# Second head mixing in four 64x64 quarters with one op a visit, and three single PSUM banks for scores, mixing and values

## The chip, the cores and the metric

The kernel runs on one core of one Trainium2 chip. The metric is the device time of one execution in microseconds, from three executions. One more execution was profiled; all rows below come from its trace. TensorE runs the matrix products (PE in the rows, with its weight loads as PEld), VectorE is DVE, ScalarE is ACT, GpSimd is POOL, and SyncE (SP) issues the DMAs.

## The reference, cut to what matters

Talking-heads attention over 4 batches, 12 heads, 448 tokens and head size 64, then two dense layers. The change touches the attention alone.

```
scores = scale * np.matmul(q, k.transpose(0, 1, 3, 2))
scores = np.einsum('bhij,hg->bgij', scores, w_pre)
scores = scores - np.max(scores, axis=-1, keepdims=True)
attn = np.exp(scores)
attn = attn / (np.sum(attn, axis=-1, keepdims=True) + 1e-09)
attn = np.einsum('bhij,hg->bgij', attn, w_post)
return np.matmul(attn, v).astype(np.float32)
...
h = x @ w_in
g = h * np.cos(h)
return (g @ w_out).astype(np.float32)
...
h = np.maximum(np.maximum(x @ w1, x @ w2), x @ w3)
return (h @ w_out).astype(np.float32)
```

The heads are mixed twice, before the softmax with w_pre (here the first mixing) and after it with w_post (the second mixing).

## The kernel before, in words

The 448 query rows of a batch are cut into four score blocks of 100, 120, 120 and 108 rows (110 with padding), so there are 16 score blocks in all. For each block `qk` (line 674) makes the scores of a pair of heads as two products in the two halves of TensorE's rows; `evac` copies each head from PSUM to a tile `s` (6 of them), and `send` moves it by DMA into the tile `t` (2 of them), where the rows of 12 heads lie together: 60 partitions (5 query rows x 12 heads) in each half of the partitions. `new_t` first fills the 4 spare partitions with zeros by a DMA.

A **visit** works on two slices of `t`. `mix1` (line 701) multiplies 64x64 quarters of it with the block-diagonal `w1`; all four quarters of TensorE take one product each. The result is one or two **blocks** of 128 partitions x 448 keys (there are 92 visits, 88 with two sides and 4 with one, and 180 blocks). For each block `rowmax` (706), `soft` (711, the exponential with its row sum), `guard` (715), `recip` (719) and `wscale` (723, the small matrix `w2s` = w_post over the row sum) follow, and then `mix2` (728): the exponentials are the weights, 112 keys at a time, and `w2s` with 120 columns streams through, so that one bank `aps` of PSUM holds 4 x 120 columns, keys on the partitions. `keep` copies it into `a2`. When the two score blocks of a half batch are done, `av` (752) multiplies `a2` with the values `v`, `keepx` copies the result out, and `out` sends it to `xT` in DRAM, which the dense layers read.

PSUM has eight banks here: `ps_m` 2 (first mixing), `ps_t` 2 (second mixing), `ps_s` 2 and `ps_x` 2 (a ring of four for scores and values; a score bank from `ps_x` has the name `mps` in the rows, as a bank of `ps_m` has). `qk` and `av` are planned two pairs of heads at a time.

No order is written by hand. Class `Plan` takes every step with a rank, the engines that may do it with a time that the author gives it, the steps it needs, and the rings of buffers it takes; `Plan.run` goes through time with these figures and so fixes the order of each engine's instructions and, for copies, whether ACT or DVE does them. Each engine then works strictly in that order. A changed figure, rank or ring changes the order of everything in the attention.

Of the kernel before, what the change touches and what calls it, by code (L numbers as in the profile page):

```python
# [21 lines left out]
RI = 10  # L22
# [7 lines left out]
BUFS = {"k": 10, "q": 9, "s": 6, "e": 4, "w2s": 3, "v": 7, "xs": 3, "a2": 2, "ps_m": 2, "ps_t": 2, "ps_s": 2, "ps_x": 2}  # L30
# [481 lines left out]
class Plan:  # L512
# [17 lines left out]
    def run(self, places):  # L530
# [8 lines left out]
        while open_:  # L539
            best = {}  # L540
            for key in open_:
                rank, run, engines, after, takes, _ = self.ops[key]
                t = max([done[x] for x in after], default=-50.0)
                for ring in takes:
                    if len(taken[ring]) >= places[ring]:
                        last = self.frees[ring, taken[ring][-places[ring]]]
                        t = max([t] + [done.get(x, 1e9) for x in last])
# [15 lines left out]
            for ring in takes:  # L563
                taken[ring].append(key)
# [17 lines left out]
def attention(ctx, tc, q, k, v, w_pre, w_post, same_row, xT, tp, mlps):  # L582
# [8 lines left out]
        pool("v", BUFS["v"]), pool("xs", BUFS["xs"]), pool("a2", BUFS["a2"]))  # L591
# [11 lines left out]
    own = const.tile([128, RH], F32, name="own")  # L603
    zero = const.tile([PAD, S], F32, name="zero")
    w1 = const.tile([128, 64], F32, name="w1")
    w2t = const.tile([128, H, RI], F32, name="w2t")
    for x in (zero, wraw, blk, w1):
        nc.vector.memset(x, 0.0)

# [18 lines left out]
    def wmix(x, _):  # L628

        w = wraw[:, x, :]  # L630
        if x == 0:
            nc.vector.tensor_scalar(w, w, 1.0 / math.sqrt(D), None, op0=ALU.mult)
            nc.vector.tensor_add(own, blk[:, 0, :RH], blk[:, 0, RH:])
            nc.vector.tensor_mul(
                w1[:, :PH].rearrange("p (r g) -> p r g", g=H), w.unsqueeze(1).to_broadcast([128, RH, H]),
                own.unsqueeze(2).to_broadcast([128, RH, H]))
        else:
            nc.vector.tensor_mul(
                w2t, w.unsqueeze(2).to_broadcast([128, H, RI]), blk[:, 1, :].unsqueeze(1).to_broadcast([128, H, RI]))
# [11 lines left out]
    def vget(b, hp, _):  # L651
        live["v", b, hp] = vp.tile([JC, JB, 2, D], F32, name="v")
        nc.sync.dma_start(live["v", b, hp], v[b, hp])


    def pairs(x):
        return 2 * x, 2 * x + 1
# [9 lines left out]
    def qk(n, x, _):  # L667
        b, i0, m, _ = score[n]
        for hp in pairs(x):
            both = [score_psum(), score_psum()]  # L670
            for g, ps in enumerate(both):
                half = slice(64 * g, 64 * g + 64)
                live["s", n, 2 * hp + g] = ps
                nc.tensor.matmul(ps[:m], live["q", b, hp][half, i0:i0 + m], live["k", b, hp][half], start=True, stop=True)  # L674
# [18 lines left out]
    def mix1(v, _):  # L693
        n, u, sides = visits[v]
        i = blocks.index((n, u, 0))
        for a in sides:
            live["m", i + a] = ps_m.tile([128, S], F32, name="mps")
        for y in range(2):
            for a in sides:
                k = slice(64 * a, PAD + (a + 1) * PH)  # L700
                nc.tensor.matmul(live["m", i + a][64 * y:64 * y + 64], w1[k], live["t", n][k, 2 * u + y, :],  # L701
                                 start=True, stop=True)

    def rowmax(i, _):
        nm = live["nm", i] = st.tile([128, 1], F32, name="nm")
        nc.vector.tensor_reduce(nm, live["m", i], axis=AX.X, op=ALU.max, negate=True)  # L706

    def soft(i, _):
        e = live["e", i] = ep.tile([128, S], F32, name="e")
        z = live["z", i] = st.tile([128, 1], F32, name="z")  # L710
        nc.scalar.activation(e, live["m", i], AF.Exp, bias=live["nm", i], scale=1.0, accum_out=z)  # L711

    def guard(i, _):
        z = live["z", i]
        nc.vector.tensor_scalar(z, z, 1e-9, None, op0=ALU.add)

    def recip(i, _):
        rz = live["rz", i] = st.tile([128, 1], F32, name="rz")
        nc.vector.reciprocal(rz, live["z", i])
# [15 lines left out]
    def keep(i, eng):  # L735
        n, u, a = blocks[i]
        half = n // 2
        if ("a2", half) not in live:
            live["a2", half] = ap_.tile([JC, JB, H, NHALF], F32, name="a2")
        hi = score[n][3][1]  # L740
        o = (n % 2) * score[n - 1][2] + 2 * u * RH + (a * RH * hi if 2 * u < hi else RH * hi)
        copy(eng, live["a2", half][:, :, :, o:o + RI], live["a", i][:JC])


    def av(n, x, _):
        m, a2 = score[n - 1][2] + score[n][2], live["a2", n // 2]
        for hp in pairs(x):
            vt = live["v", score[n][0], hp]
            ps = live["av", hp] = score_psum()
            for j in range(JB):  # L750
                for g in range(2):
                    nc.tensor.matmul(ps[64 * g:64 * g + 64, :m], vt[:, j, g, :], a2[:, j, 2 * hp + g, :m],  # L752
                                     start=j == 0, stop=j == JB - 1)

    def keepx(n, hp, eng):
# [4 lines left out]
        for x in (n - 1, n):  # L760
            _, i0, m, (lo, hi) = score[x]
            o = i0 - half_of(n)[0]
            for halves, nt in ((2, hi), (1, lo - hi)):
                m = halves * RH * nt
                if nt:
                    copy(eng, xs[:, o:o + m].rearrange("p (a r t) -> p a r t", r=RH, t=nt),
                         ps[:, c:c + m].rearrange("p (a t r) -> p a r t", r=RH, t=nt))
# [6 lines left out]
    before, visit = {}, {}  # L774
# [15 lines left out]
    for n in range(NS):  # L790
        b = score[n][0]
        start, end = n % per == 0, n % per == per - 1
        for x in range(HP // 2):
# [362 lines left out]
```

## Time and profile before

| what | value |
|---|---|
| time, median of 3 executions | 1344.89 us (1341.59 to 1346.52) |
| profiled execution, its own time | 1346.08 us |
| its span, first to last instruction | 1344.3 us |
| PE busy | 94% of the span |
| DVE busy | 72% |
| ACT busy | 48% |
| granted TensorE clock, mean | 0.972 |

The kernel has two parts. The attention takes the first 530 us or so. After that the dense layers run, with PE busy all the time. A busy PE is no PE at its peak: a product counts as busy until its last result is out, while the next one already streams.

### The profile page before, as it was taken

The numbers are of one execution on the slowest core, as the hardware profiler recorded it, in microseconds if no ns is written. First come the engines' busy times: TensorE is split into PE (matmuls) and PEld (weight loads), VectorE is DVE, ScalarE is ACT, GpSimd is POOL, SyncE is SP. The second block draws the span as 40 slices with busy tenths as digits, with TensorE's granted clock in tenths as the row PEclk, the third lists the DMA queues.
The fourth block names the chain that finished last, engine by engine and source line by source line (L and its number), as shares of the span: only waits on it lengthen the run. The fifth ranks groups of instructions, "written<-read, shape, count | busy, mean of one in ns | idle before, by whom it ended". The sixth has DMA issues, their size and how long they took to land.

```text
span 1344.3 us, 20559 instructions
## 1 busy us (share of the span) xinstructions
PE 1266.5 (94%) x7182; PEld 1007.6 (75%) x7182; DVE 964.9 (72%) x2167; ACT 650.2 (48%) x1452; POOL 187.9 (14%) x170
## 2 busy tenths in 40 slices
PE   5889998999899887899999999999999999999998
PEld 2455555555556555699999999999999998989998
DVE  1565665667475669699999999999786544956455
ACT  2444453445344456577456555555554444344440
POOL 0000000000000012100000000000105645266450
PEclk7889999899899999899999999999999999999999
DMA  5744354435225333555444444444101212222112
GB/s 167 197 132 121 93 163 118 125 100 162 85 79 149 102 128 111 167 160 142 118 131 128 119 130 139 120 124 122 42 1 59 73 52 77 85 80 83 48 53 83
DMA packets 86031, 146.83 MB, mean 109 GB/s; under 512 B 9672, under 2 KB 68904, under 8 KB 85928
## 3 DMA queue, kind: packets, MB, share of 16 engines
q1 hardware_dynamic: 85928, 145.52, 37.1%
q8 instruction: 57, 0.93, 0.3%
q14 instruction: 46, 0.38, 0.1%
HBM read 84.96 MB, written 20.45 MB: 78 GB/s over the span
## 4 chain that ended last, share of the span: by engine, by line
PE 78%; DMA 9%; DVE 4%; ACT 3%; issue 2%; SPq 2%; POOL 1%; ACTq 0%; DVEq 0%; POOLq 0%
PE ps L165 18%; PE ps L167 18%; PE ps L166 18%; PE aps L728 10%; DMA t<-s 6%; PE mps L701 6%; PE ps L752 3%; PE mps L752 2%; PE ps L674 2%; PE mps L674 2%; ACT e L711 1%; POOL w L309 1%; DMA wf<-w 1%; DMA x<-xT 1%; DVE nm L706 1%
## 5 line engine op out<-in xcount | busy, mean ns | idle before, releaser
L165 PE MATMUL ps<-x,w 128*128 128x448 f32 x708 | 262.5, 371 | 7.1 <-ACT x L152 4.2
L167 PE MATMUL ps<-x,w 128*128 128x448 f32 x708 | 260.6, 369 | 2.2 <-DVE x L156 1.6
L166 PE MATMUL ps<-x,w 128*128 128x448 f32 x708 | 260.6, 368 | 0.0
L728 PEld LDWEIGHTS aps<-w2s,e 128*112 128x112 f32 x1440 | 166.2, 185 | 113.9 <-issue 57.9
L309 POOL TENSOR_TENSOR w<-wf,w 128x384 fp32r<-128x384 f32 x126 | 141.9, 1148 | 549.0 <-DVE wt L264 370.4
L728 PE MATMUL aps<-w2s,e 128*112 128x120 f32 x1440 | 194.3, 284 | 14.9 <-DVE w2s L723 9.4
L165 PE MATMUL ps<-gh,w 128*128 128x448 f32 x528 | 193.7, 367 | 0.0
L166 PE MATMUL ps<-gh,w 128*128 128x448 f32 x528 | 193.5, 366 | 0.0
L167 PE MATMUL ps<-gl,w 128*128 128x448 f32 x528 | 193.2, 366 | 0.0
L711 ACT ACTIVATE e<-mps,nm 128x448 f32<-128x448 f32 x180 | 112.6, 630 | 114.2 <-DVE nm L706 114.1
L706 DVE TENSOR_REDUCE nm<-mps 128x1 f32<-128x448 f32 x180 | 104.3, 619 | 67.8 <-PE mps L701 67.7
L165 PEld LDWEIGHTS ps<-x,w 128*128 128x128 f32 x708 | 133.9, 189 | 24.8 <-ACT x L152 5.0
L167 PEld LDWEIGHTS ps<-x,w 128*128 128x128 f32 x708 | 133.9, 189 | 15.2 <-DVE x L156 2.4
L166 PEld LDWEIGHTS ps<-x,w 128*128 128x128 f32 x708 | 133.9, 189 | 11.2
L701 PE MATMUL mps<-t,w 64*64 64x448 f32 (+1 forms) x720 | 111.1, 600 | 26.9 <-ACT e L711 26.9
L298 DVE TENSOR_TENSOR wf<-wf 128x384 f32<-128x384 f32 x72 | 58.0, 817 | 72.0 <-POOL w L309 43.0
L167 PEld LDWEIGHTS ps<-gl,w 128*128 128x128 f32 x528 | 99.1, 188 | 9.0
L165 PEld LDWEIGHTS ps<-gh,w 128*128 128x128 f32 x528 | 99.1, 188 | 8.8
L166 PEld LDWEIGHTS ps<-gh,w 128*128 128x128 f32 x528 | 99.1, 188 | 8.6
L306 ACT CAST w<-wf 128x384 fp32r<-128x384 f32 x126 | 60.7, 512 | 91.7 <-DVE wf L298 39.9
L929 DVE TENSOR_TENSOR acc<-ps,acc 128x448 f32<-128x448 f32 x168 | 100.7, 617 | 3.3 <-PE ps L167 3.3
L156 POOL TENSOR_TENSOR x<-x 128x448 fp32r<-128x448 f32 x10 | 12.4, 1255 | 537.4 <-DMA wraw<-in_w_in_dram 499.6
(98 smaller groups left out, 1779.9 us busy)
## 6 DMA issues: line engine op xcount, KB each, us to landing
t<-s SPq DMA_DIRECT2D x96, 210.0 KB
wf<-w SPq DMA_DIRECT2D x96, 192.0 KB
wraw<-in_w_out_dram SPq DMA_DIRECT2D x44, 384.0 KB
t<-s SPq DMA_DIRECT2D x96, 175.0 KB
wraw<-in_w_dram SPq DMA_DIRECT2D x36, 384.0 KB
wraw<-in_w_in_dram SPq DMA_DIRECT2D x32, 384.0 KB
w<-wf SPq DMA_DIRECT2D x48, 192.0 KB
q<-in_q_dram SPq DMA_DIRECT2D x48, 112.0 KB
```

The costliest lines, as they stand in the source:

```text
L165: mm(w[0], x[0], start=first, stop=False)
L166: mm(w[1], x[0], start=False, stop=False)
L167: mm(w[0], x[1], start=False, stop=last)
L298: eng(raw[x], raw[l], raw[r])
L306: return nc.scalar.copy(A[x][0], w())
L309: return nc.gpsimd.tensor_sub(A[x][1], w(), f32(A[x][0]))
L701: nc.tensor.matmul(live["m", i + a][64 * y:64 * y + 64], w1[k], live["t", n][k, 2 * u + y, :], start=True, stop=True)
L706: nc.vector.tensor_reduce(nm, live["m", i], axis=AX.X, op=ALU.max, negate=True)
L711: nc.scalar.activation(e, live["m", i], AF.Exp, bias=live["nm", i], scale=1.0, accum_out=z)
L728: nc.tensor.matmul(ps[:JC, j], live["e", i][:, j * JC:(j + 1) * JC], live["w2s", i], start=True, stop=True)
L752: nc.tensor.matmul(ps[64 * g:64 * g + 64, :m], vt[:, j, g, :], a2[:, j, 2 * hp + g, :m], start=j == 0, stop=j == JB - 1)
L929: return nc.vector.tensor_add(acc, po, acc) if fg else nc.scalar.copy(acc, po)
```

## The change

Second mixing: the contraction is cut into two row halves (`y`, 60 of 64 rows) and the keys into two column halves (`c`, 64 of 112 keys, which overlap by 16), so that each product is 64x64 with 60 columns of `w2s`, and four of them stand in the four quarters. One `mix2` step does a whole visit: 4 key pieces x 2 sides x 2 halves x 2 halves = 32 products instead of 2 x 4. Its two results lie in two banks, one for each `y`, so a step takes both banks of `ps_t`. `guard`, `recip` and `wscale` work on both sides at once. The keys of `a2` and `v` are spread over 128 partitions, with 16 zero rows in `v`: the seven `v` tiles are made once and zeroed by GpSimd, and each load of `v` is two DMAs.

Buffers: `ps_m` 3 instead of 2, taken and freed bank by bank; `ps_s` 1 instead of 2, so scores and values share three banks; `e` 5 instead of 4. `qk` and `av` are planned one pair of heads at a time. Planner figures and ranks change with them. The `av` of the last half batch takes only the one bank of `ps_s`.

```diff
-BUFS = {"k": 10, "q": 9, "s": 6, "e": 4, "w2s": 3, "v": 7, "xs": 3, "a2": 2, "ps_m": 2, "ps_t": 2, "ps_s": 2, "ps_x": 2}
+BUFS = {"k": 10, "q": 9, "s": 6, "e": 5, "w2s": 3, "v": 7, "xs": 3, "a2": 2, "ps_m": 3, "ps_t": 2, "ps_s": 1, "ps_x": 2}
...
+    places = [vp.tile([128, JB, 2, D], F32, name=f"v{x}") for x in range(BUFS["v"])]
...
+    for x in places:
+        nc.gpsimd.memset(x, 0.0)
...
     def vget(b, hp, _):
-        live["v", b, hp] = vp.tile([JC, JB, 2, D], F32, name="v")
-        nc.sync.dma_start(live["v", b, hp], v[b, hp])
...
+        live["v", b, hp] = places[(b * H // 2 + hp) % len(places)]
+        for a in range(2):
+            to, of = a * (128 - JC // 2), a * JC // 2
+            nc.sync.dma_start(live["v", b, hp][to:to + JC // 2], v[b, hp][of:of + JC // 2])
...
-    def wscale(i, eng):
-        w2s = live["w2s", i] = wp.tile([128, H, RI], F32, name="w2s")
-        any_of[eng].tensor_scalar(w2s, w2t, live["rz", i], None, op0=ALU.mult)
-
-    def mix2(i, _):
-        ps = live["a", i] = ps_t.tile([128, JB, H, RI], F32, name="aps")
+    def wscale(v, _):
+        sides = len(visits[v][2])
+        w2s = live["w2s", v] = wp.tile([128, 2, H * RH], F32, name="w2s")
+        shape = [128, sides, H * RH]
+        nc.vector.tensor_mul(w2s[:, :sides], w2t.rearrange("p g r -> p (g r)").unsqueeze(1).to_broadcast(shape),
+                             live["rz", v].unsqueeze(2).to_broadcast(shape))
+
+    def mix2(v, _):
+        for y in range(2):
+            live["a", v, y] = ps_t.tile([128, JB, H, 2, RH], F32, name="aps")
         for j in range(JB):
-            nc.tensor.matmul(ps[:JC, j], live["e", i][:, j * JC:(j + 1) * JC], live["w2s", i], start=True, stop=True)
+            for a in visits[v][2]:
+                for y in range(2):
+                    k = slice(64 * y, 64 * y + PH)
+                    for c in range(2):
+                        o = j * JC + c * (JC - 64)
+                        nc.tensor.matmul(live["a", v, y][64 * c:64 * c + 64, j, :, a, :], live["e", v, a][k, o:o + 64],
+                                         live["w2s", v][k, a], start=True, stop=True)
...
-            add(qk, (n, x), r, {"T": 1.98}, [(f, b, hp) for f in ("qget", "kget") for hp in pairs(x)], turn=True, takes=["ps"] * 4,
-                frees=[(f, (f + "get", b, hp)) for f in "kq" for hp in pairs(x)] if end else [])
...
+            add(qk, (n, hp), r, {"T": 0.95}, [("qget", b, hp), ("kget", b, hp)], turn=True, takes=["ps"] * 2,
+                frees=[(f, (f + "get", b, hp)) for f in "kq"] if end else [])
...
-        add(mix2, (i,), i + 1.5, {"T": 0.82}, [key("wscale")], turn=True, takes=["ps_t"], frees=[("e", key("soft")), ("w2s", key("wscale"))])
...
+        add(mix2, (y,), i + 1.5, {"T": 0.15 + 0.45 * m}, [key("wscale")], turn=True, takes=["ps_t"] * 2,
+            frees=[("e", key("soft", a)) for a in sides] + [("w2s", key("wscale"))])
...
-            add(av, (n, x), r, {"T": 3.25}, [("vget", b, hp) for hp in pairs(x)] + ends, turn=True, takes=["ps"] * 2,
-                frees=[("a2", start)] + [("v", ("vget", b, hp)) for hp in pairs(x) if n // 2 % 2])
...
+            add(av, (n, hp), r, {"T": 1.7}, [("vget", b, hp)] + ends, turn=True, takes=[ring],
+                frees=[("a2", start)] + [("v", ("vget", b, hp))] * (n // 2 % 2))
```

What the planner makes of it, first on PE, in the middle of the third batch, where visits alternate with the scores of the next block (a product of `qk` is L674 before and L677 after, `mix1` L701 and L703, `mix2` L728 and L742). Before:

```order
L674 MATMUL ps<-k,q 100x448 x2
L728 MATMUL aps<-w2s,e 112x120 x4
L701 MATMUL mps<-t,w_133 64x448 x4
L728 MATMUL aps<-w2s,e 112x120 x4
L674 MATMUL mps<-k,q 100x448 x2
L674 MATMUL ps<-k,q 100x448 x2
```

And of the change, at the same place:

```order
L677 MATMUL ps<-k,q 100x448
L677 MATMUL mps<-k,q 100x448
L742 MATMUL aps<-w2s,e 64x12x5 x32
L703 MATMUL mps<-t,w_133 64x448 x4
L677 MATMUL mps<-k,q 100x448
L677 MATMUL ps<-k,q 100x448
```

Before, a visit had one `mix1`, two separate `mix2` of 4 products and two pairs of heads (4 products of `qk`); now it has one `mix1`, one `mix2` of 32 products and one pair of heads, whose two scores lie in two of three banks by turns.

On DVE, at a visit there, before (`rowmax` L706, `keep` and `evac` L597, `guard` L715, `recip` L719, `wscale` L723):

```order
L706 TENSOR_REDUCE nm<-mps 128x1 x2
L597 COPY a_2270<-aps 112x48x10
L715 TENSOR_SCALAR z<-z 128x1
L719 RECIPROCAL rz<-z 128x1
L715 TENSOR_SCALAR z<-z 128x1
L723 TENSOR_SCALAR w2s<-w2t,rz 128x120
L719 RECIPROCAL rz<-z 128x1
L723 TENSOR_SCALAR w2s<-w2t,rz 128x120
L597 COPY s<-mps 100x448
L597 COPY s<-ps 100x448
```

And of the change, at a visit of the same kind (`rowmax` L708, copies L599, `guard` L719, `recip` L724, `wscale` L730):

```order
L719 TENSOR_SCALAR z<-z 128x2
L724 RECIPROCAL rz<-z 128x2
L708 TENSOR_REDUCE nm<-mps 128x1
L730 TENSOR_TENSOR w2s<-w2t,rz 128x120
L708 TENSOR_REDUCE nm<-mps 128x1
L599 COPY s<-mps 100x448
L599 COPY a_2922<-aps 128x48x10
```

The six small operations of a visit became three; the two maxima of the next visit now stand around `wscale`, and one score copy stands where two stood.

## Rows read from the trace of the kernel before

**Rows 1.** Stretches of one batch each: us, then busy us (count) by engine, clock, DMA.

```profile
core 0: us, PE busy (x) PEld busy (x) DVE busy (x) ACT busy (x) POOL busy (x), PEclk, DMA share, GB/s
33.00:155.00 122.00, 109.36 (x716) 63.53 (x716) 75.04 (x231) 52.41 (x137) 0.00 (x0) 0.90 0.47 134
155.00:277.00 122.00, 112.21 (x824) 68.04 (x823) 75.92 (x242) 56.44 (x151) 0.00 (x0) 0.96 0.44 129
277.00:399.00 122.00, 111.21 (x831) 67.67 (x832) 76.60 (x244) 56.37 (x151) 0.00 (x0) 0.97 0.40 115
399.00:521.00 122.00, 108.50 (x810) 69.03 (x809) 83.45 (x249) 59.44 (x158) 10.81 (x9) 0.97 0.39 116
...
700.00:800.00 100.00, 100.00 (x492) 91.83 (x491) 98.27 (x201) 57.29 (x111) 0.00 (x0) 1.00 0.48 132
```

**Rows 2.** Chain of work that ended last within 33 to 523 us, by line.

```profile
by line: PE aps L728 26.7%; PE mps L701 16.1%; DMA t<-s 14.2%; PE ps L752 7.3%; PE mps L752 6.7%; PE ps L674 6.2%; PE mps L674 6.2%; ACT e L711 3.5%; DVE nm L706 2.7%; DMA x<-xT 1.6%; DVE w2s L723 1.6%; issue 1.5%; DVE a L597 1.0%; DVE s L5
```

**Rows 3.** That chain in order of time in the second batch: start, us, what.

```profile
226.91 0.91 PE mps L701 x8
227.82 1.00 PE aps L728 x8
228.83 3.12 PE mps L752 x32
...
233.87 0.94 PE ps L674 x4
234.81 0.75 PE mps L674 x4
235.56 1.82 PE aps L728 x16
...
248.50 5.81 DMA t<-s
```

**Rows 4.** Instructions of line 701: ns min/median/max, first and last start, forms.

```profile
L701 PEld LDWEIGHTS mps<-t,w x720: 129/132/228, 33.6 to 522.1; 64*64 64x64 f32 x155, 60*64 60x64 f32 x25
L701 PE MATMUL mps<-t,w x720: 536/587/1007, 33.6 to 522.5; 64*64 64x448 f32 x164, 60*64 60x448 f32 x16
```

**Rows 5.** Timeline from 204.9 us: start, us, engine, line; one `mix1`.

```profile
205.40 0.21 PEld L701 LDWEIGHTS mps<-t,w 64*64 64x64 f32 x8
205.41 0.98 PE L701 MATMUL mps<-t,w 64*64 64x448 f32 x8
```

**Rows 6.** Groups by line within 33 to 523 us: busy us, mean ns.

```profile
L711 ACT ACTIVATE e<-mps,nm 128x448 f32<-128x448 f32 x179 | 111.9, 630 | 113.6 <-DVE nm L706 113.5
...
L706 DVE TENSOR_REDUCE nm<-mps 128x1 f32<-128x448 f32 x179 | 103.7, 619 | 67.8 <-PE mps L701 67.7
L597 DVE COPY a<-aps 112x480 f32<-112x480 f32 x101 | 65.7, 651 | 8.7 <-PE aps L728 8.2
L723 DVE TENSOR_SCALAR w2s<-w2t,rz 128x120 f32<-128x120 f32 x178 | 53.0, 298 | 3.3
...
L719 DVE RECIPROCAL rz<-z 128x1 f32<-128x1 f32 x179 | 28.5, 159 | 2.6
...
L715 DVE TENSOR_SCALAR z<-z 128x1 f32<-128x1 f32 x179 | 26.2, 146 | 38.1 <-ACT e L711 34.6
L597 DVE COPY s<-ps 120x448 f32<-120x448 f32 (+2 forms) x41 | 25.4, 618 | 11.1 <-DMA t<-s 11.1
```

**Rows 7.** Waits of the engines within 33 to 523 us: total, times, longest.

```profile
ACT s L597 <- DMA t<-s: 57.9, 19, 6.2
...
PE mps L701 <- ACT e L711: 26.9, 19, 4.5
```

**Rows 8.** Timeline of the DMA queue of SP around 250 us.

```profile
246.67 0.75 SPq L683 DMA_DIRECT2D t<-zero  x1
247.52 12.43 SPq L691 DMA_DIRECT2D t<-s  x12
...
287.37 0.35 SPq L653 DMA_DIRECT2D v<-in_v_dram  x1
```

**Rows 9.** Timeline of PE at the end of the attention: the last six `av` pairs.

```profile
528.59 3.33 PE L752 MATMUL ps<-a,v 112*64 112x230 f32 x32 [0.75 <-DVE a L597]
533.77 6.43 PE L752 MATMUL ps<-a,v 112*64 112x230 f32 x64 [1.86 <-ACT xs L597]
```

More of the change, by code (lines that the diff above doesn't have):

```diff
@@ L665, in score_psum, with qk @@
         return ps_x.tile([128, S], F32, name="mps")
-    def qk(n, x, _):
+    def qk(n, hp, _):
         b, i0, m, _ = score[n]
[L669 to L674, printed above, removed]
+        both = [score_psum(), score_psum()]
+        for g, ps in enumerate(both):
+            half = slice(64 * g, 64 * g + 64)
+            live["s", n, 2 * hp + g] = ps
+            nc.tensor.matmul(ps[:m], live["q", b, hp][half, i0:i0 + m], live["k", b, hp][half], start=True, stop=True)
     def evac(n, h, eng):
@@ L733, in half_of, with keep, av @@
         return score[n][1], score[n + 1][1] + score[n + 1][2] - score[n][1]
-    def keep(i, eng):
-        n, u, a = blocks[i]
+    def keep(v, y, eng):
+        n, u, sides = visits[v]
         half = n // 2
         if ("a2", half) not in live:
[L739 to L745, printed above, removed]
-        m, a2 = score[n - 1][2] + score[n][2], live["a2", n // 2]
[L747 to L753, printed above, removed]
+            live["a2", half] = ap_.tile([128, JB, H, NHALF], F32, name="a2")
+        t, hi, m = 2 * u + y, score[n][3][1], RH * len(sides)
+        o = (n % 2) * score[n - 1][2] + RI * min(t, hi) + RH * max(t - hi, 0)
+        copy(eng, live["a2", half][:, :, :, o:o + m].rearrange("p j g i -> p (j g) i"),
+             live["a", v, y][:, :, :, :len(sides)].rearrange("p j g a r -> p (j g) (a r)"))
+    def av(n, hp, _):
+        m, a2 = score[n - 1][2] + score[n][2], live["a2", n // 2]
+        vt = live["v", score[n][0], hp]
+        ps = live["av", hp] = score_psum()
+        for j in range(JB):
+            for g in range(2):
+                nc.tensor.matmul(ps[64 * g:64 * g + 64, :m], vt[:, j, g, :], a2[:, j, 2 * hp + g, :m],
+                                 start=j == 0, stop=j == JB - 1)
     def keepx(n, hp, eng):
@@ L792, in attention @@
         start, end = n % per == 0, n % per == per - 1
-        for x in range(HP // 2):
-            r = (first[n - 1] + 0.5 + 3.0 * x) if n else -40.0 + 2 * x
-            for hp in pairs(x) if start else ():
+        for hp in range(HP):
+            r = (first[n - 1] + 0.5 + 1.5 * hp) if n else -40.0 + hp
+            if start:
                 early = 8.0 if b else 20.0
@@ L829, in attention @@
         last = (first + [N])[n + 1] - 1
[L830 to L840 removed]
+        ends = [("keep", y, a) for y, x in enumerate(visits) if x[0] in (n - 1, n) for a in range(2)]
+        start = ends[0]
+        for hp in range(HP):
+            r = last + 2.5 + 1.5 * hp
+            ring = "pa" if n == NS - 1 else "ps"
+            if n // 2 % 2 == 0:
+                add(vget, (b, hp), r - 10.0, {"D": 0.65}, turn=True, takes=["v"])
+            add(av, (n, hp), r, {"T": 1.7}, [("vget", b, hp)] + ends, turn=True, takes=[ring],
+                frees=[("a2", start)] + [("v", ("vget", b, hp))] * (n // 2 % 2))
+            add(keepx, (n, hp), r, {"A": 0.45, "V": 0.5}, [("av", n, hp)], turn=True, takes=["xs"], frees=[(ring, ("av", n, hp))])
+            add(out, (n, hp), r, {"D": 0.45}, [("keepx", n, hp)], turn=True, frees=[("xs", ("keepx", n, hp))])
     FG = mlps.GROUPS
@@ L1013, in first_layer @@
                 tags = ["k"] * (y == 0) + ["r"] * (y == 2) + ["gh", "gl"] * (y == 6 and i == 0)
-                after = [("act", s, i, y - 1) if y else ("hidden", s, i, KC - 1)] + [("soft", x) for x in range(N)] * (s == 0 and y == 4)
+                after = [("act", s, i, y - 1) if y else ("hidden", s, i, KC - 1)] + [("soft", y, a) for y, x in enumerate(visits) for a in x[2]] * (s == 0 and y == 4)
                 if i and y == 6:
```

109 lines of the change are left out of this document (52 added, 57 removed).

## The prediction, made before the changed kernel ran

> **What bounds the kernel now.** I read first the stretches of one batch each, 122 us from 33 to 521 us: PE is busy for 108 to 112 of the 122, DVE for 75 to 83, ACT for 52 to 59, and after the attention PE is busy all the time [rows 1]. So the change can only pay in the first 530 us. Second the chain of work that ended last in these 490 us: the second mixing carries 26.7% of it (131 us), the first 16.1%, values 14.0%, scores 12.4%, and the landing of `t<-s`, the heads on their way into `t`, 14.2% (70 us) [rows 2]. Third the same chain in order of time, which gives each burst's price with the change to the next shape of product in it: a `mix1` 0.91 us, a lone `mix2` 1.00, two in a row 1.82, two pairs of `qk` 0.94 + 0.75, two pairs of `av` 3.12 [rows 3].
>
> With these prices a batch of 23 visits and 45 blocks is: `mix1` 23 x 0.91 = 20.9; `qk` 12 x 1.69 = 20.3; `av` 6 x 3.12 = 18.7; `mix2` 45 x 0.96 (between 0.91 and 1.00) = 43.2. Together 103.1 us of PE, and 18.9 of the 122 in which PE stands still. Most of those belong to `t<-s`, 70 / 4 = 17 a batch: a score copy waits in ACT's strict order for one of the six `s` (57.9 us in 19 waits) and the exponentials behind it wait too, and with them `mix1` (26.9 us) [rows 2, 7]. PE is the bound in most of the stage and the sends are in the rest.
>
> **The change part by part.** *Second mixing.* Two in a row cost 0.82 more than one and stand as 8 more instructions in the trace (a product in float32 stands there as two), so 0.1025 us for 120 columns, and the change of shape is 1.00 - 0.82 = 0.18 [rows 3]. A two-sided visit now has 32 products, 64 instructions, in 16 rounds of four quarters with 60 columns each: half of 0.1025 is 0.051 a round, if four quarters run at once and the loads hide. That they do is seen in the first mixing, the same quarters: eight products of at least 0.536 end within 0.98 us of the first's start, and eight loads of 0.13 lie within 0.21, so two rounds of loads start within 0.08 [rows 4, 5]. I take 0.056 a round: 16 x 0.056 + 0.18 = 1.08, say 1.1 a visit and 0.65 for the one-sided one. The bounds: 1.0 from 0.051, and 1.82 if a round costs as much as one of 120 columns does now. No overlap at all (64 x 0.051 = 3.3) is excluded by the same rows.
>
> The Trainium skill has a rule against this (TensorE: Matmul & The Clock Gate, section "Wait — 56ns, not 53.3ns?"): start-to-start of products does not fall below some 25 ns however few the columns. By it a visit would be 64 x 25 ns = 1.6 us and 0.18. The trace disagrees for products in different quarters: eight loads start within 0.08 us [rows 5].
>
> A batch is then `mix2` 22 x 1.1 + 0.65 = 24.9; `mix1` 20.9; `qk` 24 single pairs at 0.94 = 22.6 (each now pays its own change of shape, 0.19 twelve times); `av` 12 at half of 3.12 and half of the 0.18, 1.65, = 19.8. Together 88.2 us: 14.9 less.
>
> *Small operations.* On DVE a block's guard, reciprocal and scaling are 0.146 + 0.159 + 0.298 = 0.60 us, 45 x 0.60 = 27 a batch [rows 6]. Now 23 times, on two or 120 columns; the first two have so few columns that I keep their price, and the product of two tensors on 120 columns, unseen here, lies between the 0.146 of a column and the 0.619 of 448 [rows 6]; I take 0.30, nearest to the 120-column row. That frees 13 us of DVE a batch, off PE's path, so nothing is counted. But in a visit with one pair of heads PE has 0.91 + 0.94 + 1.1 = 2.95 us, and DVE two maxima 1.24, the three small operations 0.61, one `keep` 0.65 and one score copy 0.62 = 3.12 [rows 6]. There DVE is as long as PE; at worst 23 x 0.17 = 4 us a batch, less where `av` fills PE. I add 2.
>
> *Three score banks, a pair at a time.* A pair needs two of three banks, so one copy must be out before the next pair's second score. A visit of 3 us gives it time; an end of it that costs is the last rival. Four heads used to come at once and met six `s`; now two come in a visit. A `t` freed by its last `mix1` gets zeros (0.75 us) and then the first head, which lands up to 5.8 us after its issue [rows 3, 8]: some 7 us in which no `s` comes free. The seventh head now stands behind three more pairs, three visits, some 9 us. I expect the stalls to fall from 18.9 to 15.5; both ends are in the range: 8 (the sends hidden) and 28 (below).
>
> *Three mixing banks.* They let the first side of a `mix1` go ahead; its second still waits for an exponential of the visit before. Counted in the stalls.
>
> *Values.* Six more DMA issues a batch at 0.35 us on SP [rows 8]; behind them stand the sends. SP has 13 issues for most blocks, 25 for the fourth, at up to 1.04 [rows 8], so it has room: nothing, at most 8 us in all. The zeroing of `v` by GpSimd lies under the first 33 us of loads, in which nothing reads `v`.
>
> *End of the attention.* The last six pairs of `av` took two banks by turns, with one wait of 1.86 for a copy [rows 9]; on one bank all five hand-overs wait. From nothing (dense products fill in) to 5 x 1.86 = 9 us; I take 3, since copies run beside.
>
> *Sum.* A batch: -14.9 + 2 - 3.4 = -16.3; four are -65; with the end -62 us. The profiled execution took 1346.08 us, span 1344.3; it lies 1.2 above the median of 1344.89. From the median: **1283 us**.
>
> **The rivals.** *The sends bound it.* The fourth block's `t` takes 25 issues, at up to 1.04 us 26 us [rows 8], and a landing; its cover is the time of the block before, and a block's mean shrinks from 122 / 4 = 30 to 106 / 4 = 26. Then PE gains and stands: stalls of 28 a batch, 88.2 + 28 = 116 of 122, and 1344.9 - 24 + 3 = 1324 us. For it: SP's order is strict and heads now leave evenly up to the last visit. Against: three of four blocks need only 13 issues.
>
> *A round of quarters costs twice the columns.* `mix2` writes runs of 5 columns at a step of 10 where it wrote 120 in a row. If that made a round as long as one of 120 columns (1.82 a visit), a batch is 88.2 + 22.5 x 0.72 = 104.4 us, PE gains nothing and the stalls' 3.4 are left: 1344.9 + 4 x (1.3 - 3.4) + 3 = 1340 us, no change. The Trainium skill speaks for it (PSUM — Partial Sum Buffer, "Specifications (TRN2)": any access to PSUM that is not contiguous slows matmuls significantly); no row here has such a product. Against it: `mix1` shows that the quarters themselves run at once [rows 4, 5], and a dense product of 448 columns takes 100 / 492 = 0.203 us [rows 1], 0.054 for 120, where these float32 ones take 0.1025, so a written column has about twice the time here.
>
> *Slower: both banks of `ps_t` at once.* Before, PE filled one bank while the other was copied. Now a `mix2` waits for both copies of the visit before. A copy is 0.65 us [rows 6], with 0.1 to start; if an exponential (0.63) stands before it, the banks are free some 1.4 to 1.6 us after the last product. Between the two lie `mix1` and a pair, 1.85 us, so nothing shows; where only the `mix1` (0.91) lies between, 0.5 to 0.7 do. PE's gain is 62 / 92 = 0.67 us a visit: from a mean wait of that size on the change loses, and at 1.0 us it is 1344.9 + 92 x 0.33 = 1375 us. The new order has a pair of heads or of values between in most places, which speaks against it.
>
> *More than forecast.* Stalls fall to 8 a batch: 88.2 + 2 + 8 = 98, 1344.9 - 95 + 3 = 1253 us.
>
> **How the numbers follow.** The forecast (1255 to 1310) has 0.58, the better case 0.08, the sends 0.14, the slow round 0.12 (of which 0.03 faster, 0.06 the same, 0.03 slower, as its 1340 lies among them), the two banks 0.08 with 0.07 of it slower and 0.01 the same. Half a per cent, 6.7 us, is about what a measurement here can tell from no change. Faster: 0.58 + 0.08 + 0.14 + 0.03 = 0.83; same 0.07; slower 0.10. The range of 8 in 10 takes in the better case and the sends and ends before the slow round's 1340: 1250 to 1338. The likeliest case's own is 1255 to 1310.
>
> **What would show it.** Right: a `mix2` of 64 instructions in 1.0 to 1.2 us on the chain; batches of about 106 us where they were 122; the chain's share of the second mixing down from 131 to about 100 us or less; waits of score copies for `t<-s` at or below 58 us. Wrong: a `mix2` near 1.8 us; `mix2` waiting for copies of `a`; PE waiting long for `t<-s`; a granted clock lower than 0.96 in these stretches, since a PE with more pauses might be given 1.2 GHz more often; then the time is beyond 1310.

## The result, and the profile after

The changed kernel takes 1263.39 us (median of four executions, 1258.51 to 1263.62) where the kernel before takes 1345.7 us (median of four on the same chip): a ratio of 0.938, 95% interval 0.935 to 0.942, 82 us less. Forecast were 1283 us, 62 less, in a range of 1250 to 1338. The profiled execution took 1263.26 us, its span 1260.7.

The instructions of `mix1`, now line 703 (us of first and last start after ns min/median/max), and then the stretches of one batch each (columns as in [rows 1]):

```profile
L703 PE MATMUL mps<-t,w x720: 536/542/1003, 36.4 to 428.0; 64*64 64x448 f32 x176, 60*64 60x448 f32 x4
```

```profile
36.00:134.00 98.00, 82.07 (x1704) 41.86 (x1705) 60.81 (x156) 51.18 (x137) 0.00 (x0) 0.91 0.59 168
134.00:232.00 98.00, 88.69 (x1835) 47.16 (x1836) 64.67 (x173) 53.59 (x147) 0.00 (x0) 0.97 0.54 156
232.00:330.00 98.00, 91.62 (x1908) 49.16 (x1900) 67.18 (x177) 55.08 (x151) 0.00 (x0) 0.98 0.50 145
330.00:428.00 98.00, 89.86 (x1907) 49.57 (x1905) 71.22 (x185) 58.88 (x158) 4.83 (x5) 0.98 0.49 146
sum 392.00, PE 352.25 PEld 187.75 DVE 263.88 ACT 218.72 POOL 4.83; mean PE 88.06 PEld 46.94 DVE 65.97 ACT 54.68 POOL 1.21
```

From the first `mix1` to the last it is 391.6 us, where it was 522.5 - 33.6 = 488.9 [rows 4]: 97.3 less, 24.3 a batch, and 98 us a batch now where 122 stood [rows 1]. By the sum line PE is busy for 352.3 us of the four batches and stands for 39.7; before, by the same reckoning, it was busy for 441.3 of 488 and stood for 46.7 [rows 1]. So of the 96 us that the four batches lost, 89 are PE's busy time and 7 its standing. Three small pieces go the other way. The stage begins 2.8 us later. From the last `mix1` to the end of the last `av` it is 27.5 us (to 455.5, in the rows of PE below), where it was 17.7 [rows 4, 9]: 9.8 more. From there to the span's end it is 805.2 us against 804.1. The sum, 2.8 - 97.3 + 9.8 + 1.1, is the -83.6 of the two spans.

The chain of work that ended last within 33 to 441 us, by line (`mix2` is L742, `mix1` 703, `av` 767, `qk` 677, the sends 694):

```profile
by line: PE aps L742 19.9%; PE mps L703 15.0%; PE mps L767 14.9%; DMA t<-s 11.9%; PE mps L677 7.7%; PE ps L677 7.5%; issue 3.4%; PE ps L767 2.9%; DMA x<-xT 2.3%; DMA xT<-xs 2.1%; SPq L694 2.1%; DVE a L599 1.5%; DVE nm L708 1.3%; DVE w2s L73
```

The second mixing has 81 us of it instead of 131, and `t<-s` 49 instead of 70 [rows 2]. That chain in order of time, at three visits of the second batch and a little later:

```profile
176.01 1.16 PE aps L742 x64
177.17 0.76 PE mps L703 x8
177.93 0.56 PE ps L677
178.49 0.37 PE ps L677
178.86 0.12 issue
178.98 1.16 PE aps L742 x64
...
181.96 1.16 PE aps L742 x64
183.11 0.97 PE mps L703 x8
...
187.94 1.64 PE mps L767 x16
189.58 1.09 PE aps L742 x64
...
194.49 1.64 PE mps L767 x16
196.13 0.91 PE mps L703 x8
...
206.35 3.20 PE mps L767 x16
```

A visit with a pair of heads takes 2.97 us, and all but 0.12 of it is PE. `mix2` is 1.16 us there and 1.09 behind an `av`. `mix1`, which was 0.91 [rows 3], is 0.76 where it follows a `mix2` without a pause: it then begins about 0.2 us before the `mix2` has ended, and behind other bursts only 0.07 before. Where it waits until the `mix2` is over, as at 183.11, it is 0.97. Of its 94 bursts in the trace, 52 begin early in this way. Both are now products of the same 64x64 shape; that a change of shape is saved here is a reading that no run tests.

Waits within 33 to 441 us (total, times, longest):

```profile
DVE a L599 <- PE aps L742: 51.5, 68, 3.2
...
DVE s L599 <- DMA t<-s: 18.8, 8, 7.4
ACT s L599 <- DMA t<-s: 17.1, 7, 6.4
DVE xs L599 <- DMA xT<-xs: 14.0, 3, 7.3
...
PEld mps L703 <- ACT e L714: 5.0, 6, 3.2
...
PE mps L703 <- ACT e L714: 2.4, 1, 2.4
...
PEld aps L742 <- ACT a L599: 1.9, 1, 1.9
...
PEld aps L742 <- DVE a L599: 0.2, 1, 0.2
```

The exponentials' queue on ACT is held 17.1 us by score copies that wait for an `s`, where it was 57.9, and the products of `mix1` wait 2.4 us for an exponential where they waited 26.9 [rows 7]. Their weight loads (PEld) wait 5.0 us for one, where before it was:

```profile
PEld mps L701 <- ACT e L711: 39.9, 45, 4.7
```

That is a change of the waits, not of PE's work, and most of the experiments turn on it. Waits of different engines lie beside each other, though: their sums are not time that PE lost.

The last six `av` (timeline of PE; in brackets the idle time before, and what ended it):

```profile
439.63 1.77 PE L767 MATMUL ps<-a,v 128*64 128x230 f32 x16
442.74 1.77 PE L767 MATMUL ps<-a,v 128*64 128x230 f32 x16 [1.33 <-DVE xs L599]
446.07 1.77 PE L767 MATMUL ps<-a,v 128*64 128x230 f32 x16 [1.56 <-ACT xs L599]
448.55 1.77 PE L767 MATMUL ps<-a,v 128*64 128x230 f32 x16 [0.70 <-ACT xs L599]
451.26 1.77 PE L767 MATMUL ps<-a,v 128*64 128x230 f32 x16 [0.94 <-ACT xs L599]
453.74 1.77 PE L767 MATMUL ps<-a,v 128*64 128x230 f32 x16 [0.70 <-ACT xs L599]
```

All five hand-overs of the one bank wait, 5.2 us together.

### The profile page after: what moved, and what is told of

Same layout as the page of the kernel before. It is cut to its first block, busy times and chain, and to the rows that moved or that the text cites. A ratio compares the mean times of both kernels' runs of the same rounds, so it can differ in the third digit from the quotient of the medians.

```text
span 1260.7 us, 28927 instructions
## 1 busy us (share of the span) xinstructions
PE 1184.6 (94%) x11502; PEld 930.1 (74%) x11502; DVE 923.7 (73%) x1893; ACT 650.8 (52%) x1464; POOL 196.5 (16%) x180
## 4 chain that ended last, share of the span: by engine, by line
PE 77%; DMA 9%; DVE 6%; issue 3%; SPq 2%; POOL 2%; ACT 1%; DVEq 0%; ACTq 0%; POOLq 0%
PE ps L165 18%; PE ps L167 18%; PE ps L166 18%; PE aps L742 6%; PE mps L703 5%; PE mps L767 5%; DMA t<-s 4%; PE mps L677 3%; PE ps L677 3%; DMA wf<-w 2%; POOL w L309 2%; DVE wf L298 2%; PE ps L767 1%; DMA wraw<-in_w_in_dram 1%; SPq L655 1%
## 5 line engine op out<-in xcount | busy, mean ns | idle before, releaser
L742 PEld LDWEIGHTS aps<-w2s,e 60*64 60x64 f32 x5760 | 96.9, 137 | 70.5 <-issue 53.5
L708 DVE TENSOR_REDUCE nm<-mps 128x1 f32<-128x448 f32 x180 | 108.4, 616 | 29.7 <-PE mps L703 28.1
L742 PE MATMUL aps<-w2s,e 60*64 60x60 f32 x5760 | 109.1, 223 | 15.9 <-DVE w2s L730 11.0
L677 PE MATMUL mps<-k,q 64*120 64x448 f32 (+2 forms) x242 | 104.7, 633 | 2.2 <-DMA k<-in_k_dram 2.1
L703 PE MATMUL mps<-t,w 64*64 64x448 f32 x720 | 95.4, 564 | 10.0 <-DMA t<-s 6.0
```

The source lines that it names most:

```text
L703: nc.tensor.matmul(live["m", v, a][64 * y:64 * y + 64], w1[k], live["t", n][k, 2 * u + y, :], start=True, stop=True)
L708: nc.vector.tensor_reduce(nm, live["m", v, a], axis=AX.X, op=ALU.max, negate=True)
L742: nc.tensor.matmul(live["a", v, y][64 * c:64 * c + 64, j, :, a, :], live["e", v, a][k, o:o + 64], live["w2s", v][k, a], start=True, stop=True)
```

## The experiments

Ratios are to the kernel before, measured on the same chip; its medians beside the runs were 1345 to 1346 us.

### Which part gives how much

**Rings without quarters.** The kernel before with three mixing banks, three score banks and one pair of heads at a time, the second mixing unchanged. The planner also takes and frees banks one by one, as in the changed kernel, and the last `av` keep to one bank.

```diff
-"e": 4, ... "ps_m": 2, "ps_t": 2, "ps_s": 2, "ps_x": 2
+"e": 4, ... "ps_m": 3, "ps_t": 2, "ps_s": 1, "ps_x": 2
...
-            add(qk, (n, x), r, {"T": 1.98}, ... takes=["ps"] * 4,
+            add(qk, (n, hp), r, {"T": 0.95}, ... takes=["ps"] * 2,
```

> The kernel before with only the other division of PSUM: three mixing banks, three banks for scores and values, one pair of heads at a time, the planner's ring bookkeeping by bank; the second mixing and the small operations stay as before. If TensorE's time in the second mixing carries the gain: 1340 to 1360 us, since PE has the same products and pays twelve more changes of shape of 0.19 us a batch for scores and six for values (14 us in all) against what stalls shrink. If the banks and the smoother order carry it: below 1320 us.

1296.28 us, ratio 0.964 (0.961 to 0.967): 49 us less without any change of PE's products. Its chain within 33 to 476 us:

```profile
by line: PE aps L729 37.8%; PE mps L702 19.1%; PE mps L752 14.7%; PE ps L675 9.4%; PE mps L675 8.6%; DMA t<-s 2.9%; PE ps L752 1.1%; DVE nm L707 1.1%; ACT e L712 0.9%; issue 0.9%; DVE a L599 0.7%; DVE w2s L724 0.5%; ACT a L599 0.4%; DVE rz 
```

`t<-s` is down from 70 us to 13, and PE is the bound nearly everywhere. Four batches of it:

```profile
sum 434.00, PE 420.17 PEld 249.63 DVE 296.69 ACT 236.56 POOL 8.28; mean PE 105.04 PEld 62.41 DVE 74.17 ACT 59.14 POOL 2.07
```

PE stands for 13.8 us, where it stood for 46.7 before. The changed kernel has these rings and the quarters: PE's busy time falls by another 68 us, to 352, and PE stands for 39.7 again. So the quarters took from PE nearly the 73 us that the prediction's prices have for `mix2` (43.2 - 24.9 a batch), and over a third of it came back as standing.

**Quarters without rings.** The changed kernel with the four old rings and two pairs of heads at a time. It keeps the fifth `e`, the planner's figures and the freeing of single banks.

```diff
-"e": 5, ... "ps_m": 3, "ps_t": 2, "ps_s": 1, "ps_x": 2
+"e": 5, ... "ps_m": 2, "ps_t": 2, "ps_s": 2, "ps_x": 2
...
-            add(qk, (n, hp), r, {"T": 0.95}, ... takes=["ps"] * 2,
+            add(qk, (n, x), r, {"T": 1.98}, ... takes=["ps"] * 4,
```

> The changed kernel with PSUM divided as before (two mixing banks, four banks for scores and values, two pairs of heads at a time). If TensorE's time in the second mixing carries the gain: 1262 to 1285 us. If the banks carry it: above 1305 us. With both needed (two mixing banks hold a visit back once PE is faster): 1285 to 1305 us.

1328.84 us, 0.989 (0.986 to 0.992): 16 us less, as its second reading has it. Rings 49 and quarters 16 make 65; together they give 82, and behind the rings the quarters are worth 33. The two parts are not independent, so the rings were split. The fifth `e` and the planner's figures were not tried by themselves.

**Single pairs without the third mixing bank**, once on the kernel before and once on the changed one:

```diff
 (the kernel before)
-            add(qk, (n, x), r, {"T": 1.98}, ... takes=["ps"] * 4,
+            add(qk, (n, hp), r, {"T": 0.95}, ... takes=["ps"] * 2,
```

> The kernel before with pairs of heads planned one at a time for scores and values, and every bank as before (two mixing banks, four for scores and values). The three other parts together gave -49 us. If four heads at once overfilling the six s is what stalled it, this alone gives most of that: 1295 to 1315 us, and waits of score copies for t fall from 73 us to below 30. If the third mixing bank did it: 1335 to 1350 us and those waits stay.

```diff
 (the changed kernel)
-"ps_m": 3, "ps_t": 2, "ps_s": 1, "ps_x": 2
+"ps_m": 2, "ps_t": 2, "ps_s": 2, "ps_x": 2
```

> The changed kernel with two mixing banks and four for scores and values, pairs one at a time: only the third mixing bank is taken back. If pairs one at a time carry the gain: 1262 to 1275 us. If the third mixing bank does, since a first mixing with two banks waits for both exponentials and each visit then takes 2.5 to 3.1 us at least: 1295 to 1325 us.

1306.37 us, 0.973 (0.970 to 0.976), and 1335.83 us, 0.994 (0.992 to 0.996). With the old second mixing single pairs give 39 us, and the bank moved from scores to mixing another 10. The first time is as expected, but not by the expected wait: score copies still wait 56 us for `t<-s` (73 before), not under 30. With quarters that bank is worth 72, and 1336 us lies above both ranges expected: single pairs without the third mixing bank are even 7 us slower than two pairs at a time (1329). The first two batches of the changed kernel with single pairs and the old rings, and the sum of all four:

```profile
36.00:156.00 120.00, 97.62 (x1824) 50.06 (x1816) 65.04 (x163) 56.72 (x148) 0.00 (x0) 0.86 0.48 140
156.00:276.00 120.00, 103.77 (x1865) 54.82 (x1868) 68.27 (x176) 55.69 (x149) 0.00 (x0) 0.88 0.44 130
...
sum 480.00, PE 406.68 PEld 217.35 DVE 281.56 ACT 229.75 POOL 9.70; mean PE 101.67 PEld 54.34 DVE 70.39 ACT 57.44 POOL 2.43
```

PE has the same products as in the changed kernel, and a batch takes 120 us instead of 98. PE stands more, 73 us of the four batches instead of 40, but it is also busy for 54 us longer. The granted clock (PEclk), the share of its full 2.4 GHz that TensorE is given, is 0.86 to 0.88 in these two stretches against 0.91 to 0.97. It has two levels, and at the lower one, 1.2 GHz, the same burst takes about twice as long: in the changed kernel an `av` is 3.20 us on the chain at 206.35, where the granted clock is 0.50, and 1.64 elsewhere.

**Seven banks.** Moving a bank changes two rings. So one run takes the third mixing bank away and puts nothing in its place.

```diff
-"ps_m": 3, "ps_t": 2, "ps_s": 1, "ps_x": 2
+"ps_m": 2, "ps_t": 2, "ps_s": 1, "ps_x": 2
```

> The changed kernel with two mixing banks instead of three and nothing in place of the third: three score banks as in the changed kernel, one bank of PSUM idle. It parts the two readings of the 1336 us that quarters_single_pairs gave, which had two mixing banks and four score banks. Theory A, the mixing bank itself: a mix1 of two sides can't begin before both exponentials of the visit before are out, so each visit holds that wait whatever the scores do: 1325 to 1350 us, PE waiting for e some 35 us, idle time of PE in the stage near 100 us. Theory B, the fourth score bank did the harm: with four banks the planner puts several pairs of heads between two visits, they meet six s at once, and copies that wait for t<-s hold the exponentials behind them on ACT; with three score banks that is gone: 1262 to 1285 us, t<-s waits of ACT near 17 us instead of 90.

1313.25 us, 0.976 (0.973 to 0.980): between the two theories. Without the third mixing bank it is 50 us slower, and the fourth score bank makes it 23 slower still: a bank more, and a slower kernel. Its waits within 33 to 485 us:

```profile
ACT s L599 <- DMA t<-s: 62.6, 22, 9.1
...
DVE s L599 <- DMA t<-s: 50.2, 27, 8.1
...
PEld mps L703 <- ACT e L714: 22.1, 39, 1.8
```

The bank's own wait, that of the weight loads of `mix1` for an exponential, grew by 17 us, which is the kind of wait that theory A names, but the waits of ACT and DVE for an `s` grew by 77 together. Its chain, in order of time, at the last `mix1` of a block, and the queue of SP there:

```profile
250.01 1.10 PE aps L742 x64
...
253.79 0.99 PE mps L703 x4
...
255.59 6.25 DMA t<-s
...
261.86 0.54 ACT s L599
...
262.45 1.84 PE ps L677 x2
```

```profile
254.80 0.70 SPq L686 DMA_DIRECT2D t<-zero  x1
255.59 11.39 SPq L694 DMA_DIRECT2D t<-s  x10
```

The timeline of PE there:

```profile
262.45 1.84 PE L677 MATMUL ps<-k,q 64*120 64x448 f32 x2 [3.11 <-ACT s L599]
```

Six heads of the next block had been copied already and filled the six `s`. The `mix1` at 253.79 frees their `t`; zeros go out at 254.80, the sends from 255.59, and the seventh copy starts at 261.86. It is the same piece of the chain as the 5.81 us that the kernel before shows at 248.50 [rows 3, 8]. PE still has products of visits already begun in most of it, and stands for 3.1 us at its end; then, from 262.1 to 268.9, the granted clock is 0.50. In the trace I counted how many of a block's 12 copies start before the last `mix1` of the block that holds its `t`, for the 14 blocks from the third on, and set it beside the time, and beside what PE does in four batches:

| kernel | blocks with six copies too early | median us | four batches, us | PE stands | mean granted clock |
|---|---|---|---|---|---|
| before | 8 | 1345 | 488 | 47 | 0.95 |
| single pairs, old mixing | 2 | 1306 | 446 | 23 | 0.96 |
| rings, old mixing | 0 | 1296 | 434 | 14 | 0.97 |
| quarters, two pairs | 8 | 1329 | 470 | 71 | 0.90 |
| quarters, single pairs, two mixing and four score banks | 11 | 1336 | 480 | 73 | 0.88 |
| seven banks | 8 | 1313 | 444 | 56 | 0.92 |
| the changed kernel | 0 | 1263 | 392 | 40 | 0.96 |

```profile
sum 444.00, PE 387.54 PEld 205.40 DVE 288.14 ACT 214.68 POOL 6.93; mean PE 96.89 PEld 51.35 DVE 72.04 ACT 53.67 POOL 1.73
```

That is seven banks. With the same second mixing, more such blocks mostly go with more time. Eight times the 6.25 us of the piece above would even be the 50 us between seven banks and the changed kernel, and nearly the 49 between before and rings. But PE stands only 17 us more in the four batches with seven banks, of 52; the other 35 are longer busy time for the same products. The clock makes part of that: a mean of 0.92 in 444 us is 72 us at the lower level, against 31 in the changed kernel, and at half speed that loses some 20 us more (an estimate). The rest is not split. Quarters with two pairs at a time have as many such blocks as seven banks and are 16 us slower, so the count alone does not set the time. It was made after the runs; it is a reading that fits most of the rows, and no test.

### The remaining terms

**Small operations apart.** Guard, reciprocal and scaling once for each side again.

```diff
-        add(recip, (y,), i, {"V": 0.12}, [key("guard")])
-        add(wscale, (y,), i, {"V": 0.25}, [key("recip"), ("wmix", 1)], turn=True, takes=["w2s"])
+            add(recip, (y, a), i, {"V": 0.08}, [key("guard", a)])
+            add(wscale, (y, a), i, {"V": 0.2}, [key("recip", a), ("wmix", 1)], turn=True, takes=["w2s"] * (a == 0))
```

> The changed kernel with guard, reciprocal and scaling done for each side by itself again, 0.60 us of DVE for each side in place of 0.61 for both. If DVE's freed 13 us a batch lie beside PE's work: 1261 to 1272 us. If DVE is as long as PE in the visits, so that merging carried part of the gain: 1280 to 1300 us.

1264.92 us, 0.942 (0.938 to 0.946): no difference from the changed kernel that this can show, though the three small operations take 99 us of DVE within 33 to 441 us there and 57 in the changed kernel. So the merging is worth nothing that shows here, and DVE is not the bound.

**Order of the products.** The same 32 products of a `mix2`, one quarter after another instead of by turns.

```diff
-        for j in range(JB):
-            for a in visits[v][2]:
-                for y in range(2):
-                    k = slice(64 * y, 64 * y + PH)
-                    for c in range(2):
+        for y in range(2):
+            for c in range(2):
+                for j in range(JB):
+                    for a in visits[v][2]:
+                        k = slice(64 * y, 64 * y + PH)
```

> The changed kernel with the same 32 products of a visit in another order: all of one quarter, then all of the next, in place of one of each by turns. If a quarter's products only overlap when neighbours in the order lie in other quarters: a second mixing of 64 x 0.058 = 3.7 us, 92 x 2.6 = 240 us more at most, 1400 to 1500 us. If each quarter is fed by itself whatever the order: 1.1 to 1.3 us and 1260 to 1280 us.

1405.71 us in one execution, slower than before. Its chain within 90 to 130 us:

```profile
98.89 3.32 PE aps L742 x64
102.22 1.64 PE mps L767 x16
```

By turns, a `mix2` is 1.09 to 1.16 us; quarter by quarter 3.32, which is 0.052 us an instruction. In this kernel quarters run at once only where neighbours in the order lie in different quarters.

**Columns in a row.** A product's 60 columns are written in a row of the bank, not as 12 runs of 5 at a step of 10, in two-sided visits. They land at other places of the bank, so heads are mixed up in the result; the work is the same.

```diff
-                        nc.tensor.matmul(live["a", v, y][64 * c:64 * c + 64, j, :, a, :], live["e", v, a][k, o:o + 64],
+                        to = live["a", v, y][64 * c:64 * c + 64, j]
+                        to = to.rearrange("p g a r -> p (g a r)")[:, a * H * RH:(a + 1) * H * RH] if len(visits[v][2]) > 1 else to[:, :, a, :]
+                        nc.tensor.matmul(to, live["e", v, a][k, o:o + 64],
```

> The changed kernel, whose mix2 writes its 60 columns of a product as 60 columns in a row of the bank, where it wrote 12 runs of 5 at a step of 10 (two-sided visits alone). The columns so land at other places of the bank, and the output is that of a kernel that mixes up columns; the work is the same. Theory A (an access to PSUM with a step costs nothing here): a round stays 0.058 us, mix2 1.09 to 1.16 us on the chain, 1258 to 1268 us. Theory B (the steps slow the product): a round falls toward 0.051 or below, mix2 to 1.0 us or less, 92 times 0.1 to 0.16, 9 to 15 us: 1248 to 1255 us.

1261.19 us, 0.938 (0.935 to 0.940): theory A. On its chain `mix2` is 1.16 us in the visits with a pair of heads, as in the changed kernel. The instructions of `mix2` in it, and then in the changed kernel:

```profile
L744 PE MATMUL aps<-w2s,e x5760: 209/218/359, 41.6 to 435.8; 60*64 60x60 f32 x199
```

```profile
L742 PE MATMUL aps<-w2s,e x5760: 209/218/360, 43.1 to 438.1; 60*64 60x60 f32 x199
```

**The last `av` in the three mixing banks**, which are free by then.

```diff
-        ps = live["av", hp] = score_psum()
+        ps = live["av", hp] = ps_m.tile([128, S], F32, name="mps") if n == NS - 1 else score_psum()
...
-            ring = "pa" if n == NS - 1 else "ps"
+            ring = "ps_m" if n == NS - 1 else "ps"
```

> The changed kernel with the last six pairs of values in the three mixing banks in place of the one score bank. The trace shows five waits of 0.70 to 1.56 us between them, 5.2 us together, and the loads of the dense layers' weights stand behind their outputs in SP's order. If that is on the path: 1256 to 1260 us. If other work hides it: 1261 to 1265 us.

1258.18 us, 0.936 (0.933 to 0.938). Its interval overlaps that of the changed kernel, so the 5.2 us between the medians (3.6 by the two ratios) are not sure. PE there:

```profile
440.77 7.99 PE L767 MATMUL mps<-a,v 128*64 128x230 f32 x80
450.42 1.77 PE L767 MATMUL mps<-a,v 128*64 128x230 f32 x16 [1.65 <-DVE xs L599]
```

Of the five waits, 5.2 us together, one of 1.65 is left, for an `xs`: 3.6 us less. That fits the first reading, without proving it.

**More `s`, more `xs`.** The changed kernel with eight `s`, and with five `xs`.

```diff
-"s": 6, ... "xs": 3
+"s": 8, ... "xs": 3
```

> The changed kernel with eight s tiles for the heads on their way to t, in place of six. The chain of the changed kernel has 12% on the landing of t. If the six tiles hold it back: 1235 to 1255 us. If what holds is the time of the sends themselves behind a freed t: 1258 to 1268 us.

```diff
-"s": 6, ... "xs": 3
+"s": 6, ... "xs": 5
```

> The changed kernel with five tiles xs instead of three. The copies of values out of PSUM wait 14.0 us in 3 waits for an xs whose transfer to xT stands behind the sends in SP's order. Theory A (these waits set the end of their visits, since keepx holds a score bank): 14 us less at most, 1249 to 1258 us. Theory B (the place of that wait is taken by another, as with eight s): within 0.5% of the changed kernel, 1257 to 1268 us, the chain's share of DMA xT<-xs gone and another's up.

1260.61 us, 0.938 (0.934 to 0.941), and 1262.47 us, 0.938 (0.936 to 0.940): neither does anything that shows alone. With eight `s` the waits change places; its chain within 33 to 440 us, where `t<-s` had 11.9% and `xT<-xs` 2.1%:

```profile
by line: PE aps L742 21.0%; PE mps L703 16.6%; PE mps L767 12.3%; PE mps L677 9.1%; PE ps L677 8.3%; DMA t<-s 6.3%; DMA xT<-xs 4.3%; PE ps L767 3.6%; issue 3.6%; SPq L694 3.0%; DMA x<-xT 2.3%; DMA q<-in_q_dram 1.7%; DVE a L599 1.5%; DVE w2s
```

That six `s` suffice here agrees with the table above, where the changed kernel has no block left that fills them too early.

**All together**: the last `av` in mixing banks, eight `s`, five `xs`.

> The changed kernel with the last six av in the three mixing banks, eight s and five xs: every buffer that was found short, together. Theory A (each short ring took another's place, so that only all together help): stage waits for t<-s and xT<-xs both under 5 us each, 1240 to 1250 us. Theory B (the order and PE's own work set the stage now): only the 5 us of the last av stay, 1255 to 1261 us.

1249.71 us (1247.15 to 1254.26), 0.929 (0.927 to 0.931), the fastest version of this study, 14 us below the changed kernel, with intervals that don't meet. Its chain within 33 to 429 us:

```profile
by line: PE aps L742 22.2%; PE mps L703 18.4%; PE mps L767 13.9%; PE ps L677 9.8%; PE mps L677 9.4%; DMA t<-s 6.9%; PE ps L767 3.8%; issue 3.1%; SPq L694 2.5%; DMA x<-xT 2.2%; DVE a L599 1.2%; DMA v<-in_v_dram 0.9%; DMA k<-in_k_dram 0.8%; D
```

`xT<-xs` is gone from the front of it, and `t<-s` has 27 us of it instead of 49. The time is at the upper end of theory A's range, but its sign did not come: score copies still wait 32 us for `t<-s` (18 on ACT, 15 on DVE; 36 in the changed kernel), not under 5. Whether the two rings help only together is not shown either: the three edits alone are 2.8, 0.9 and 5.2 us by their medians, 9 of the 14, and each of these has an interval of some 3 to 5 us to either side.

## Why the prediction was right

The sign and the range held, and so did the prices of PE's bursts; the gain was 20 us larger than forecast, and its stalls did not behave as the sum has them. From the first `mix1` to the last it is 97 us less where 65 were forecast, 32 more; beginning and end together cost 14 us where 3 were taken, which gave 11 of the 32 back. That two misses went opposite ways is luck: without the second the time would lie near 1253, at the edge of the range. By its own steps:

- **Quarters.** `mix2` was forecast at 1.1 us a visit within 1.0 to 1.82, and is 1.09 to 1.16. If a change of shape is 0.15 us (0.91 - 0.76), a round is (1.09 - 0.15) / 16 = 0.059 us, where 0.056 was taken. The rival of a slow round is dead: whole bursts near 1.8 us stand on the chain only at the lower clock (1.98 at 66.27 and 1.91 at 307.13, granted 0.50 there), and columns in a row change nothing. The 3.3 us without any overlap, which the prediction excluded, is what the order quarter by quarter takes (3.32). The Trainium skill's statement (PSUM — Partial Sum Buffer, "Specifications (TRN2)") that access to PSUM that is not contiguous slows matmuls isn't borne out by these float32 writes, 0.938 of before with steps and without. The Trainium skill's floor of some 25 ns between starts (TensorE: Matmul & The Clock Gate, "Wait — 56ns, not 53.3ns?") isn't a floor for products in different quarters either: 64 instructions in 1.09 us are 17 ns each.
- **Pairs and values.** Forecast 0.94 and 1.65; measured 0.93 to 0.95 and, for most `av`, 1.64.
- **`mix1`.** Held at 0.91; it is 0.76 right behind a `mix2`. This saving was not in the sum: 52 bursts x 0.15 / 4 = 2.0 us a batch.
- **DVE.** Two us a batch were added because a visit has 3.12 us of DVE against 2.95 of PE. Steady visits take 2.97, and undoing the merge costs nothing. The term should have been nothing. The `wscale` of 120 columns took 294 ns, as taken.
- **Stalls, the term that was mis-sized.** 18.9 us a batch were to become 15.5. By PE's prices a batch now has 88.2 us of PE, less the 2.0 above; of its 98 us, 11.8 are left over, 7.1 less where 3.4 were forecast. But what the prices leave over is not all time "in which PE stands still", as the prediction calls it. Its own rows give PE's standing as 46.7 us in four batches, 11.7 a batch and not 18.9 [rows 1], and it fell only to 9.9. The rest of the 18.9 is busy time above the prices, which were read from bursts at the higher clock. That is where most of the surprise lies: PE's busy time fell by 89 us in four batches where its prices fell by 60, and by 68 with the saving of `mix1`. Time at the lower clock fell from 49 to 31 us (by the mean granted clocks of 0.95 and 0.96), some 9 us at half speed; the other 12 are not split.
- **Rings and quarters.** The prediction had the place right (heads that meet six `s`, and a `t` that is not free) but took the rings as a small help beside PE's gain. Experiments show that rings alone bring 49 us and quarters alone 16. Rings take most of PE's standing away (47 us to 14 in four batches); quarters then shorten its work and bring standing back (40). And the third mixing bank, "counted in the stalls", is worth 50 us once quarters are there.
- **Why that bank weighs more with quarters** is shown only in part. Shown: without it ACT and DVE wait 77 us more for `t<-s`, and the loads of `mix1` 17 us more for an exponential; the order copies six heads before their `t` is free in 8 blocks instead of none; and of the 52 us that four batches are longer, 17 are PE's standing and 35 its busy time, part of it by a lower clock. That the planner then lets heads go ahead because `mix1` must wait for both exponentials of the visit before, is argued from its rules. Eight `s` in the seven-bank kernel would have tested it and wasn't tried.
- **End of the attention.** Forecast 3 within 0 to 9. It is 9.8 more. The five waits are 5.2 us of it, and a run that removes 3.6 of them is 3.6 to 5.2 us faster, within its noise. The other 4.6 are not split by a run, and neither are the 2.8 us by which the stage begins later, which the sum does not have.
- **The other rivals.** The sends did not bound it through SP's issues, but through the heads' order they nearly took all of the gain in the versions with two mixing and four score banks (1329 to 1336, beside the 1324 of that rival). The weight loads of `mix2` wait for copies of `a` only 2.1 us in two waits, and its products not at all, so the two `ps_t` banks cost nothing that shows. The better case, stalls of 8 at 1253 us, is near the time of the version with all rings mended (1250), with its batches down from 98 us to 95. Of the signs of being wrong, a granted clock under 0.96 stood in the first stretch (0.91), as it had before (0.90), so it told nothing.

## What to carry to other kernels

Cutting a small product into quarters pays if neighbours in the instruction order lie in different quarters, and pays little where the freed engine then waits: here quarters brought 16 us with the old rings and 33 with the new ones. Before giving a buffer ring one more place, look at what the order puts ahead of what: a fourth score bank made this kernel 23 us slower, and with it heads filled the six `s` before their `t` was free in 11 blocks instead of 8. Rings that each look worthless alone are worth one run together: here it was 14 us faster, though that they help only together was not shown. And time left over by prices is not all standing: count busy time, standing and clock apart.

## What was unexpected in the hardware

- Two bursts of the same quarter shape overlap more here than two of different shapes: `mix1` is 0.76 us right behind `mix2`, 0.91 to 0.98 behind others or after a pause.
- Products with 60 columns in different quarters follow each other at 17 ns on the mean (64 in 1.09 us), in the same quarter at 52 ns (64 in 3.32 us).
- In these traces a PE that stands more also has the lower clock, although it has the same products: of four batches it stands 40 us at a mean granted clock of 0.96 in the changed kernel, 56 at 0.92 with seven banks, 73 at 0.88 with single pairs and the old rings.
